# Moving all sums of g and of w_out's halves to GpSimd, and placing every step of a fused attention and PReLU kernel anew

## The chip, the cores and the metric

The kernel runs on one core of a Trainium2 chip. The core has five engines that run side by side, each through its own instructions in order: TensorE (PE in the profile, with its weight loads as PEld), VectorE (DVE), ScalarE (ACT), GpSimd (POOL) and SyncE (SP, which only issues DMAs here). The metric is the time of one execution on the device in microseconds (us); less is better.

## What is computed

There are 8 batches and 8 heads, 512 tokens and 32 states per head, with vectors of 64. Tokens read from states, states read from tokens (both by softmax), and all rows, 4096 of tokens and 256 of states, each 512 long over the heads, go through a two-layer network with a PReLU of its own slope for each of the 2048 hidden units.

```
scores = scale * x @ state^T            # per batch and head: 512 x 32
a      = softmax(scores);   xread = a @ state
a2     = softmax(scale * state @ x^T);  sread = a2 @ x
rows   = concatenate([xread, sread])    # heads side by side: 4352 x 512
h      = rows @ w_in                    # w_in: 512 x 2048
g      = max(h, 0) + alpha * min(h, 0)
out    = g @ w_out                      # w_out: 2048 x 512
```

Inputs and outputs are float32; the matrix products take float16.

## The kernel before

**Order.** The instructions are in an order that is written out by hand: the string ORDER (lines 17 to 95) holds 1090 tokens, and the loop at line 735 runs them one after another. A token is the name of a step and its arguments, split by dots, and the table at line 720 says which function it calls. The tiles' framework adds the waits that the data and the buffers need. As each engine runs its instructions in the order in which they were written, the order of the tokens is the order on every engine and in every DMA queue: a step that has to wait holds up what stands behind it on its engine. Where a step can run on several engines, a letter in the token says which: `a` ACT, `v` DVE, `p` POOL. A last number in a token of a matrix product is the PSUM bank (0 to 5) that it opens; a new owner of a bank waits until the old content is read. Two more banks, "two", hold scores or a pair of state-by-w_in products.

**Loads.** x of batch 0 comes in two float32 halves over SP's queue (`load_x0`), the states of batch 0 over ACT's, and alpha behind x on SP's. The others go over POOL's queue and are cast to float16 on the way: `lst` the other states, `wi.f` a quarter of w_in, `wo.i` a quarter of w_out, `lx.b` x of batch b (three buffers). `stc` casts the states of batch 0 on POOL.

**Attention, batch by batch.** For batch 0, x is cast (`cx`) and transposed by PE (`xt`, copied out by `xo`); `tsc` makes the scores of its tokens, with the states in pairs (`sbd`). For the others `xd` transposes x by a DMA of SP's queue (batch 1 goes by `xt`), `sc` makes the scores with the states on the partitions, and `sb` transposes them in blocks. The softmax over states is `smax` (DVE), `ssh` (subtracts the maximum; DVE or POOL), `sexp` (ACT), `ssum` (DVE), `snorm` (POOL), and `wb` turns the weights back (batch 0: `at` and `ao`). The softmax over tokens is `tm` (maximum, DVE), `nb` (scales the maximum, ACT or DVE), two `te` (ACT), `tsum` (DVE), two `tn` (POOL), `tt` (a DMA transpose), and `rd` with `rdo`, which read the tokens into the row block of the states.

**First layer.** The reads of the states are not made for themselves: `m.b.f` multiplies the states of batch b by a quarter f of w_in (`mo` casts it out of PSUM), and `F.b.j` multiplies that by the softmax weights: h for 512 tokens and 128 hidden units (batch 0 begins in halves, `f`). The rows of the states are batch 8, with w_in itself. `N` (ACT) takes relu(-h), and `G` (DVE) adds (1 - alpha) times it to h, which gives g; `n` and `g` are the same for `f`. `oma` makes 1 - alpha on DVE.

**Second layer.** Batches 0 to 2 multiply g by w_out outright: `S.b.q.j`, two hidden blocks for 128 tokens, into one bank; `O` copies and stores. Batches 3 to 8 use seven products of halves instead of eight (a Strassen form). `W.i` makes four sums ws of w_out's halves, `U.b.i.c` makes four sums of g's halves for each of two groups c of hidden units (16 blocks of 128 units are 4 groups; a sum is 128 x 1024, and 128 x 512 in batch 8), and `P.b.p.i.c` multiplies for one row half i. The products run together in three banks x, y and v; `K` keeps what stands in x, and `Q` adds it and stores a quarter. U.b.1.c feeds P.b.5, U.b.2.c feeds P.b.6 and U.b.4.c, U.b.3.c feeds P.b.7, and U.b.4.c feeds P.b.3. Each sum of g has one buffer, so the next batch's sum waits for the last product of this one.

`Z.k.n` issues n products of zeros, which compute nothing.

Of the kernel before, what the change touches and what calls it, by code (L numbers as in the profile page):

```python
# [22 lines left out]
tsum.0 tn.0.1 tn.0.0 ao.1.v n.0.1.0 xt.1.1.0.4 n.0.0.0 g.0.1.0.1 F.0.4.1 g.0.0.0.0 xt.1.1.1.2 g.0.1.0.0 mo.1.0.a  # L23
xt.1.0.0.3 m.1.1 N.0.4 xo.1.1.1.v S.0.2.1.5 xt.1.0.1.2 xo.1.0.0.a xo.1.1.0.v mo.1.1.a g.0.0.0.1 S.0.2.0 m.2.0.3.4
xo.1.0.1.v sc.1 G.0.4 mo.2.0.a.0 f.0.1.1.0 tm.1 mo.2.0.a.1 f.0.0.1.2 n.0.1.1 F.0.7.1 F.0.5.3 g.0.1.1.0 n.0.0.1 F.0.6.4
g.0.1.1.1 W.1.p nb.1.a te.1.1 g.0.0.1.0 g.0.0.1.1 S.0.1.1.0 S.0.1.0 S.0.3.0.2 S.0.3.1 N.0.5 sb.1 te.1.0 N.0.6 G.0.5
m.0.2 mo.0.2.a N.0.7 G.0.6 S.0.1.2 S.0.2.2 smax.1 ssh.p.1 S.0.3.2 F.0.10.3 N.0.10 F.0.9.4 G.0.7 m.0.3 G.0.10 N.0.9
S.0.2.3 mo.0.3.a F.0.8.1 F.0.11.3 N.0.8 G.0.9 S.0.1.3 N.0.11 G.0.8 S.0.3.3 sexp.1 G.0.11 F.0.12.4 ssum.1 N.0.12 G.0.12
xd.2 m.1.2 F.0.14.1 S.0.3.4 F.0.13.3 N.0.14 S.0.1.4 tsum.1 S.0.2.5 S.0.1.5 mo.1.2.a S.0.3.5 N.0.13 G.0.13 S.0.0.1.4
S.0.2.4 snorm.p.1 G.0.14 F.0.15.3 tt.0 tn.1.1 wb.1 m.1.3 N.0.15 S.0.1.6 S.0.2.6 G.0.15 F.1.10.1 S.0.1.7 F.1.4.3  # L30
S.0.2.7 mo.1.3.a W.3.p N.1.10 O.0.1.v G.1.10 N.1.4 sc.2 O.0.2.a rd.0.0 rdo.0.a G.1.4 m.2.2.1.5 S.0.3.7 sb.2 tn.1.0
tt.1 lx.3 mo.2.2.a.0 F.1.9.3 S.0.3.6 tm.2 nb.2.v N.1.9 F.1.1.0 O.0.3.a F.1.11.1 S.0.0.7 N.1.11 F.1.8.2 mo.2.2.a.1
N.1.8 G.1.9 G.1.11 N.1.1 smax.2 S.0.0.3 F.1.5.3 N.1.5 F.1.6.5 S.0.0.4 S.0.0.6 S.0.0.5 N.1.6 G.1.1 ssh.p.2 F.1.2.1
F.1.3.0 te.2.1 G.1.5 G.1.8 S.1.1.2.3 te.2.0 N.1.2 S.1.1.5 G.1.6 F.1.0.2 sexp.2 G.1.2 ssum.2 tsum.2 tn.2.0 S.0.0.0
tn.2.1 S.0.0.2 N.1.3 S.1.1.4 rd.1.5 N.1.0 O.0.0.a m.3.2 mo.3.2.a F.1.7.1 N.1.7 S.1.0.4.4 snorm.p.2 G.1.0 S.1.0.5 W.2.p
F.1.15.2 G.1.3 S.1.1.1 G.1.7 N.1.15 F.1.12.0 rdo.1.v F.1.14.1 G.1.15 N.1.12 G.1.12 S.1.1.3 xd.3 N.1.14 G.1.14 lx.4
m.2.3.5.2 m.2.1 mo.2.1.a S.1.0.0 mo.2.3.v.0 S.1.0.3 S.1.0.2 wb.2 m.3.3.0.1 mo.2.3.a.1 sc.3 mo.3.3.a.1 m.3.0.5.2
mo.3.3.a.0 mo.3.0.a.0 S.1.1.7 tm.3 F.1.13.1 N.1.13 F.2.8.0 S.1.0.1 nb.3.a G.1.13 S.1.3.0.5 S.1.0.7 sb.3 S.1.1.6
mo.3.0.a.1 te.3.0 F.2.14.2 te.3.1 tt.2 S.1.1.0 N.2.14 F.2.3.1 smax.3 O.1.1.a S.1.3.4 N.2.8 tsum.3 G.2.14 S.1.0.6
O.1.0.a F.2.1.3 ssh.p.3 G.2.8 m.3.1 N.2.3 rd.2.2 N.2.1 lx.5 F.2.12.4 rdo.2.v N.2.12 G.2.3 F.2.0.0 G.2.1 S.1.3.3 G.2.12  # L40
F.2.11.2 S.1.2.1.1 N.2.0 tn.3.0 S.1.3.2 G.2.0 N.2.11 G.2.11 sexp.3 ssum.3 snorm.p.3 tn.3.1 S.1.2.6 F.2.2.3 N.2.2 G.2.2
xd.4 F.2.15.4 F.2.6.0 N.2.15 N.2.6 F.2.5.2 N.2.5 G.2.15 G.2.5 S.1.2.7 S.1.2.2 S.1.3.6 F.2.10.3 N.2.10 G.2.6 S.1.2.5
F.2.13.4 mo.3.1.a S.1.3.5 G.2.10 m.4.1.2.0 N.2.13 mo.4.1.a.1 wb.3 tt.3 mo.4.1.a.0 S.1.3.1 S.1.2.0 S.1.3.7 m.4.0.3.0
mo.4.0.a.0 mo.4.0.a.1 O.1.3.a G.2.13 sc.4 F.2.9.2 N.2.9 S.1.2.4 F.2.7.4 S.2.1.7.3 S.2.1.5 tm.4 sb.4 N.2.7 S.2.1.0
S.2.1.6 F.2.4.0 nb.4.a te.4.1 G.2.7 G.2.9 te.4.0 S.1.2.3 smax.4 ssh.p.4 m.5.0.5.4 rd.3.2 N.2.4 mo.5.0.a.0 G.2.4
O.1.2.a lx.6 tsum.4 m.4.3 S.2.1.4 F.3.3.5 mo.4.3.v mo.5.0.a.1 F.3.7.1 N.3.3 G.3.3 S.2.1.1 N.3.7 F.3.9.0 rdo.3.a
S.2.1.2 G.3.7 N.3.9 G.3.9 S.2.1.3 tn.4.1 m.4.2.4.5 m.5.2 O.2.1.a m.7.0.2.1 mo.7.0.a.0 mo.4.2.v.1 F.3.0.0 F.3.2.3
S.2.0.2.5 N.3.0 N.3.2 S.2.0.0 sexp.4 G.3.0 mo.4.2.v.0 mo.7.0.a.1 tn.4.0 tt.4 S.2.2.1.2 F.3.15.0 N.3.15 S.2.2.4
mo.5.2.a S.2.2.3 F.3.14.4 S.2.2.6 G.3.2 ssum.4 F.3.8.1 G.3.15 F.3.1.3 N.3.14 G.3.14 snorm.p.4 S.2.0.3 xd.6 N.3.8 N.3.1
G.3.8 F.3.6.0 N.3.6 S.2.2.0 xd.5 G.3.1 F.3.5.4 m.6.0 N.3.5 F.3.4.1 G.3.6 N.3.4 F.3.10.3 N.3.10 wb.4 W.4.p F.3.11.0  # L50
N.3.11 S.2.2.2 S.2.0.1 mo.6.0.a S.2.0.6 G.3.4 S.2.2.5 rd.4.1 G.3.5 G.3.11 sc.5 rdo.4.v m.5.3.4.0 mo.5.3.a.0 mo.5.3.a.1
S.2.0.5 G.3.10 S.2.0.7 F.3.12.1 N.3.12 S.2.2.7 U.3.1.0.v S.2.3.5.4 U.3.2.0.v tm.5 nb.5.v S.2.3.3 G.3.12 S.2.3.4
F.3.13.3 N.3.13 S.2.0.4 U.3.4.0.p te.5.0 O.2.2.a S.2.3.6 te.5.1 F.4.10.0 N.4.10 F.4.9.1 S.2.3.0 O.2.0.v S.2.3.7 N.4.9
F.4.3.5 G.3.13 U.3.1.1.p S.2.3.1 F.4.13.3 P.3.1.1.1.2 S.2.3.2 sb.5 smax.5 N.4.13 P.3.1.0.1 ssh.p.5 G.4.10 O.2.3.a
F.4.4.0 G.4.9 G.4.13 F.4.11.4 N.4.3 G.4.3 tsum.5 F.4.15.1 N.4.4 tn.5.1 G.4.4 N.4.11 P.3.1.1.0 P.3.1.0.0 K.3.1.v N.4.15
F.4.6.3 F.4.12.5 N.4.6 U.3.2.1.v F.4.14.0 N.4.12 P.3.6.1.0 G.4.11 P.3.6.0.0 sexp.5 P.3.6.1.1 N.4.14 U.3.4.1.p
P.3.6.0.1 G.4.12 G.4.6 m.6.2.4.5 m.5.1 U.3.3.0.p G.4.15 mo.6.2.a.0 F.4.8.3 N.4.8 G.4.14 F.4.1.4 G.4.8 N.4.1 G.4.1
F.4.5.1 mo.6.2.a.1 P.3.2.0.0.0 K.3.2.a N.4.5 P.3.2.0.1 ssum.5 F.4.2.3 P.3.7.0.0.5 P.3.5.1.0 P.3.2.1.1 F.4.7.4
P.3.5.0.1 U.3.3.1.p P.3.2.1.0 G.4.5 F.4.0.1 N.4.2 G.4.2 P.3.7.1.0 Q.3.0.0 P.3.5.0.0 snorm.p.5 m.6.3.3.0 N.4.7 G.4.7
N.4.0 G.4.0 lx.7 mo.5.1.a P.3.5.1.1 mo.6.3.a.0 P.3.7.1.1 U.4.1.0.v mo.6.3.a.1 wb.5 P.3.7.0.1 U.4.1.1.p K.3.4.a  # L60
m.7.3.4.1 sc.6 xd.7 mo.7.3.a.0 m.6.1.3.0 mo.6.1.a.1 tm.6 P.3.3.1.0 Q.3.1.1 F.5.6.4 P.4.1.1.1.0 N.5.6 G.5.6 U.4.2.1.p
mo.7.3.a.1 P.4.1.0.1 P.3.3.0.0 sb.6 nb.6.a P.3.4.1.1 F.5.12.1 P.3.4.1.0 U.4.2.0.v mo.6.1.v.0 P.3.4.0.0 F.5.14.4
P.3.4.0.1 P.3.3.1.1 U.4.3.0.v P.4.1.0.0 te.6.1 N.5.12 Q.3.1.0 N.5.14 P.3.3.0.1 Q.3.0.1.a F.5.11.3 P.4.2.1.1.5 G.5.12
P.4.2.0.0 P.4.1.1.0 smax.6 N.5.11 G.5.11 F.5.7.1 N.5.7 G.5.14 K.4.1.v F.5.4.2 P.4.2.1.0 N.5.4 G.5.7 F.5.15.3 te.6.0
tsum.6 U.4.3.1.p ssh.p.6 U.4.4.0.p U.4.4.1.p sexp.6 P.4.2.0.1 P.4.6.0.0 G.5.4 P.4.6.1.1 sc.7 Q.4.0.0 m.7.2.4.1
mo.7.2.a.1 mo.7.2.a.0 F.5.0.2 P.4.6.0.1 P.4.6.1.0 F.5.10.5 N.5.0 ssum.6 G.5.0 P.4.7.1.0.1 F.5.3.4 N.5.15 F.5.5.2
G.5.15 K.4.2.a P.4.5.0.1 snorm.p.6 P.4.7.0.1 tm.7 P.4.5.1.0 F.5.13.3 P.4.7.1.1 N.5.5 N.5.10 G.5.10 N.5.3 P.4.5.0.0
G.5.5 N.5.13 G.5.13 wb.6 P.4.5.1.1 K.4.4.a tn.5.0 F.5.8.5 F.5.1.2 N.5.1 P.4.7.0.0 G.5.3 tn.6.1 N.5.8 P.4.3.1.0 tn.6.0
tt.6 F.6.6.3 G.5.1 P.4.3.0.0 tt.5 Q.4.1.1 F.5.9.4 F.5.2.2 N.6.6 G.6.6 U.5.1.1.p N.5.9 nb.7.a G.5.8 P.4.3.0.1 P.4.3.1.1
Q.4.0.1.a U.5.2.1.p G.5.9 N.5.2 P.4.4.1.1 F.6.0.3 m.7.1.5.0 rd.6.4 mo.7.1.a.1 mo.7.1.a.0 P.4.4.1.0 F.6.12.0 te.7.0  # L70
F.6.2.5 G.5.2 F.6.13.2 rdo.6.v U.5.3.0.p sb.7 N.6.0 te.7.1 G.6.0 N.6.12 tsum.7 P.4.4.0.1 P.4.4.0.0 Q.4.1.0 N.6.2
F.6.11.4 N.6.11 G.6.12 G.6.2 P.5.1.0.0.3 P.5.1.1.1 P.5.1.1.0 U.5.1.0.p F.6.15.1 N.6.15 P.5.2.0.1.0 N.6.13 U.5.2.0.v
# [695 lines left out]
```

## Time and profile before

| | |
|---|---|
| time, median of 3 runs | 220.82 us (220.51 to 221.13) |
| the profiled execution: its own time, its span | 220.61 us, 218.7 us |
| granted TensorE clock | 1.0 |
| bytes moved by DMA | 23.68 MB |
| sums of g on DVE and POOL (L662) | 21 and 27 |
| sums of w_out's halves on POOL (L643) | 4, mean 4071 ns |

The profile shows one execution. The span goes from the first to the last instruction of the program; the rest of the execution's time lies around it. A row of a group names line, engine, operation, output and inputs, how often, the busy us and mean ns of one, and, behind the second bar, the idle time of the engine just before them and who ended it. A row of a timeline begins with start and length in us. Busy times of PE are lengths of single matmuls, which overlap: start-to-start distances tell what PE needs. L662 is `g_sum`, L643 `w_sum`, L588 `prelu`, L585 `negative`, L532 `first`, L602 `second`, L683 `product`, L483 `state_w_in`.

### The profile page before, as it was taken

The numbers are of one execution on the slowest core, as the hardware profiler recorded it, in microseconds if no ns is written. First come the engines' busy times: TensorE is split into PE (matmuls) and PEld (weight loads), VectorE is DVE, ScalarE is ACT, GpSimd is POOL, SyncE is SP. The second block draws the span as 40 slices with busy tenths as digits, with TensorE's granted clock in tenths as the row PEclk, the third lists the DMA queues.
The fourth block names the chain that finished last, engine by engine and source line by source line (L and its number), as shares of the span: only waits on it lengthen the run. The fifth ranks groups of instructions, "written<-read, shape, count | busy, mean of one in ns | idle before, by whom it ended". The sixth has DMA issues, their size and how long they took to land.

```text
span 218.7 us, 4851 instructions
## 1 busy us (share of the span) xinstructions
PE 206.1 (94%) x1931; PEld 128.1 (59%) x1931; DVE 184.9 (85%) x282; ACT 142.7 (65%) x275; POOL 126.1 (58%) x86
## 2 busy tenths in 40 slices
...
GB/s 174 207 191 206 206 194 179 47 148 135 158 73 153 161 96 59 204 178 0 139 8 0 135 155 97 51 144 48 99 4 96 79 21 0 48 49 25 98 144 120
DMA packets 51926, 23.68 MB, mean 108 GB/s; under 512 B 38464, under 2 KB 50368, under 8 KB 51904
## 3 DMA queue, kind: packets, MB, share of 16 engines
...
q14 instruction: 7, 0.06, 0.1%
...
## 4 chain that ended last, share of the span: by engine, by line
PE 72%; DVE 13%; DMA 6%; ACT 4%; issue 2%; POOL 0%; SPq 0%; ACTq 0%; POOLq 0%
PE h L532 20%; PE px L683 15%; PE o L602 15%; PE pv L683 8%; DMA alpha_sb<-in_moe_alpha_dram 6%; PE m_ps L483 4%; DVE g L588 4%; PE py L683 3%; DVE gsum L662 2%; PE sr_ps L456 2%; PE h L541 2%; DVE ts L329 2%; ACT e L421 1%; DVE mx L362 1%; ACT neg L585 1%
## 5 line engine op out<-in xcount | busy, mean ns | idle before, releaser
L588 DVE SCALAR_TENSOR_TENSOR g<-neg,oma_sb,h 128x512 f16<-128x512 f32 (+1 forms) x140 | 93.0, 704 | 7.7 <-ACT neg L585 7.2
L585 ACT ACTIVATE neg<-h 128x512 f32<-128x512 f32 (+1 forms) x140 | 75.5, 580 | 28.6 <-PE h L532 20.5
L532 PE MATMUL h<-aT,m 128*128 128x512 f16 x248 | 68.1, 379 | 1.6 <-ACT osb L619 0.9
L602 PE MATMUL o<-w_out_sb,g 128*128 128x512 f16 x192 | 49.9, 380 | 0.0
L683 PEld LDWEIGHTS <-gsum 128*128 128x128 f16 x352 | 34.2, 98 | 9.8 <-issue 1.4
L532 PEld LDWEIGHTS <-m 128*128 128x128 f16 x248 | 23.6, 98 | 22.9 <-issue 5.0
L602 PEld LDWEIGHTS <-g 128*128 128x128 f16 x192 | 17.9, 98 | 23.2 <-issue 2.4
L683 PEld LDWEIGHTS <-g 128*128 128x128 f16 x264 | 25.7, 98 | 8.3 <-issue 1.2
L384 POOL TENSOR_TENSOR an<-ts,r 128x1024 f16<-128x1024 f32 (+1 forms) x9 | 15.5, 1722 | 20.1 <-DVE r L381 17.0
L367 POOL TENSOR_TENSOR ts<-ts,mx 128x1024 f32<-128x1024 f32 x7 | 13.4, 1912 | 23.4 <-DVE mx L362 23.4
L662 POOL TENSOR_TENSOR gsum<-g,gsum 128x1024 f16<-128x1024 f16 (+1 forms) x9 | 17.6, 1962 | 14.2 <-PE px L683 8.8
L683 PE MATMUL px<-ws,gsum 128*128 128x256 f16 x176 | 23.8, 273 | 0.2 <-DVE kept L699 0.2
L662 POOL TENSOR_TENSOR gsum<-g,g 128x1024 f16<-128x1024 f16 x6 | 13.7, 2287 | 17.1 <-DVE g L588 16.8
L509 ACT CAST m<-m_ps 128x512 f16<-128x512 f32 x32 | 17.8, 592 | 3.5 <-PE m_ps L483 3.5
L699 ACT COPY kept<-px 128x512 f32<-128x512 f32 (+1 forms) x12 | 6.9, 577 | 13.4 <-PE px L683 13.4
L662 POOL TENSOR_TENSOR gsum<-g 128x1024 f16<-128x1024 f16 (+1 forms) x7 | 13.9, 1987 | 1.8 <-DVE g L588 1.7
L421 ACT ACTIVATE e<-sc,nb 128x512 f16<-128x512 f32 x16 | 11.0, 694 | 5.0 <-issue 3.0
L483 PE MATMUL m_ps<-w_in_sb,stT 64*32 64x512 f16 x256 | 12.3, 383 | 1.3 <-ACT e L421 0.7
L435 POOL TENSOR_SCALAR e<-e,r 128x512 f16<-128x512 f16 x16 | 11.0, 697 | 4.1 <-ACT osb L619 3.1
L683 PE MATMUL py<-w_out_sb,g 128*128 128x256 f16 x88 | 12.7, 272 | 0.6 <-DVE oq L716 0.6
L507 ACT CAST m<-m_ps 128x1024 f16<-128x1024 f32 x12 | 12.2, 1017 | 1.0 <-PE m_ps L483 1.0
L683 PE MATMUL px<-w_out_sb,gsum 128*128 128x256 f16 x88 | 12.6, 273 | 0.0
...
## 6 DMA issues: line engine op xcount, KB each, us to landing
...
xg<-in_x_dram POOLq DMA_DIRECT2D x7, 512.0 KB, 8.1
...
w_in_sb<-in_moe_w_in_dram POOLq DMA_DIRECT2D x4, 512.0 KB, 11.8
w_out_sb<-in_moe_w_out_dram POOLq DMA_DIRECT2D x4, 512.0 KB, 14.7
x<-in_x_dram SPq DMA_DIRECT2D x2, 512.0 KB, 4.7
...
st<-in_state_dram POOLq DMA_DIRECT2D x1, 224.0 KB, 7.6
```

Of the source, the lines that this page charges most:

```text
L367: engine(e).tensor_tensor(blocks(cols(live["ts", b], j, S)), blocks(scored(b, j)), over_blocks(cols(live["mx", b], j, S // N)), ALU.subtract,)
L384: engine(e).tensor_tensor(blocks(cols(live["an", b], j, S)), blocks(cols(live["ts", b], j, S)), over_blocks(cols(live["r1", b], j, S // N) ...
L421: nc.scalar.activation(live["e2", b][:, g, :, :], live["sc", b][:, :, :, g, :].rearrange("p r j s -> p (r j) s"), EXP, bias=live["nb", b][ ...
L483: nc.tensor.matmul(t[N * k : N * (k + 1), :], st_head(b, h)[64 * r : 64 * r + 64, :], w_in_sb[64 * r : 64 * r + 64, c, 512 * f : 512 * (f ...
L507: copier(e)(m_tile(b, f), t)
L509: copier(e)(m_tile(b, f)[:, g, :], t[g])
L532: nc.tensor.matmul(h.rearrange("p (r j s) -> p r j s", r=2, j=2), ms[b, f][:, g, 128 * j : 128 * (j + 1)], weights(b, g), start=(g == 0), ...
L585: nc.scalar.activation(neg, h, RELU, bias=0.0, scale=-1.0)
L588: nc.vector.scalar_tensor_tensor(g_tile(b, jc), negs.pop((b, jc)), oma_sb[:, jc : jc + 1], hs.pop((b, jc)), ALU.mult, ALU.add,)
L602: nc.tensor.matmul(outs[b, q], g_tile(b, jc)[:, 128 * q : 128 * (q + 1)], w_out_sb[:, jc, :], start=not begun and jc == 2 * jc2, stop=left ...
L662: engine(e).tensor_tensor(t, x(), y(), op)
L683: nc.tensor.matmul(pbanks[b, name][:, i, :], of(b, c)[:, j, 128 * i : 128 * (i + 1)], moving[:, 4 * c + j, :], start=not begun and j == 0, ...
```

## The change

One function changes: `w_sum` makes a sum in two halves of four blocks each, so that the four W tokens become eight. The rest is in ORDER. All 48 U tokens name POOL (27 before; 21 were on DVE), as do all W. Both `nb` that were on DVE go to ACT; `ssh.6` goes from POOL to DVE; some copies change between ACT and DVE (`sto`, `cx`, `xo`, `ao`, `mo`, `rdo`, `K`, `Q`, `O`). `wi.1`, the first token before, stands behind `lx.1` now, and `wi.2`, `wi.3`, `wo.1` and `wo.2`, issued ahead of batch 0's `snorm` before, stand behind it; the first load on POOL's queue is `wi.0`, behind `stc`. Every other token may have another place and another bank. The numbers of matrix products, of zeros and of steps of the other kinds are the same.

```diff
 ORDER = """
-wi.1 stc wi.0 cx.0.0.a cx.0.1.v Z.0.9 stt.0 sbd.0.v sto.a sbd.1.a Z.1.5 lst xt.0.0.1.1 xt.0.0.0.2 Z.3.6 xo.0.0.0.v
-cx.1.1.a cx.1.0.v xt.0.1.0.3 xo.0.1.0.a xo.0.0.1.v lx.1 wo.0 tsc.0.0.4 tsc.0.1 xt.0.1.1.5 smax.0.0 ssh.v.0.0 sc.0.0
-xo.0.1.1.a m.0.1.0.2 wo.1 mo.0.1.a.0 wi.2 tsc.1.0.1 Z.3.2 tsc.1.1 smax.0.1 wi.3 wo.2 oma sc.0.1 Z.3.5 m.0.0.3.5
-sexp.0.0 Z.0.11 str.1.0 ssum.0.0 ssh.v.0.1 sexp.0.1 snorm.p.0.0 tm.0 mo.0.0.a.1 ssum.0.1 snorm.p.0.1 at.0.4 mo.0.0.v.0
-nb.0.a sro.1.a str.0.1 Z.5.13 te.0.0 ao.0.v sro.0.v f.0.1.0.5 te.0.1 f.0.0.0.0 lx.2 at.1.3 wo.3 m.1.0 mo.0.1.v.1
+stc Z.0.9 wi.0 cx.0.1.a stt.0 sto.v Z.1.5 xt.0.0.1.1 lst sbd.0.v cx.0.0.a xt.0.0.0.2 xo.0.0.0.a cx.1.0.v cx.1.1.v
+Z.3.6 xt.0.1.0.3 sbd.1.a lx.1 tsc.0.0.4 xo.0.0.1.v tsc.0.1 xt.0.1.1.5 sc.0.0 xo.0.1.1.a xo.0.1.0.v tsc.1.0.2 Z.0.2
+tsc.1.1 smax.0.0 ssh.v.0.0 sexp.0.0 smax.0.1 ssh.v.0.1 sexp.0.1 sc.0.1 tm.0 Z.0.5 m.0.0.0.1 Z.3.11 oma mo.0.0.a.0
+ssum.0.1 nb.0.a te.0.0 te.0.1 str.1.3 sro.1.a str.0.5 Z.4.13 wi.1 wo.0 snorm.p.0.1 at.1.4 ao.1.a ssum.0.0 snorm.p.0.0
+sro.0.v wi.2 mo.0.0.v.1 m.2.0.2.0 mo.2.0.v.1 wo.1 m.1.0 mo.1.0.a at.0.3 ao.0.v xt.1.1.0.5 mo.2.0.v.0 wi.3 xo.1.1.0.a
+xt.1.1.1.1 xo.1.1.1.v xt.1.0.1.4 xo.1.0.1.v f.0.1.1.0 n.0.1.1 g.0.1.1.1 xt.1.0.0.3 xo.1.0.0.v wo.2 f.0.0.0.2 n.0.0.0
+g.0.0.0.0 m.1.1 mo.1.1.a m.0.1.5.1 mo.0.1.a.0 f.0.0.1.4 mo.0.1.a.1 g.0.1.1.0 f.0.1.0.3 W.1.0.p sc.1 n.0.0.1 n.0.1.0
+g.0.0.0.1 tm.1 g.0.0.1.0 nb.1.a F.0.6.0 g.0.0.1.1 sb.1 g.0.1.0.1 N.0.6 G.0.6 g.0.1.0.0 F.0.5.2 te.1.0 lx.2 te.1.1
+S.0.1.1.5 F.0.4.1 S.0.3.1.4 wo.3 S.0.3.0 S.0.1.0 m.0.2 F.0.7.0 N.0.4 G.0.4 N.0.5 G.0.5 mo.0.2.a N.0.7 S.0.2.1.3
+S.0.2.0 G.0.7 F.0.9.1 tsum.1 tn.1.0 N.0.9 G.0.9 smax.1 ssh.p.1 xd.2 tsum.0 tn.0.1 F.0.10.2 S.0.3.3 N.0.10 G.0.10
+S.0.1.3 tn.1.1 tt.1 S.0.1.2 F.0.8.0 F.0.11.1 N.0.11 N.0.8 S.0.3.2 G.0.8 m.0.3 S.0.0.0.2 G.0.11 S.0.2.3 S.0.0.3 S.0.0.2
...
+N.8.10 P.6.3.1.1 G.8.10 F.7.6.5 N.7.6 G.7.6 P.6.7.0.0 F.7.14.2 N.7.14 P.6.7.1.1 F.8.13.4 N.8.13 Q.6.1.1 G.7.14
+P.8.1.0.1.5 P.6.2.0.0 G.8.13 P.6.4.1.0 P.6.4.0.0 P.6.2.0.1 P.7.1.0.1.2 F.8.9.4 P.6.3.0.1 P.7.1.1.0 P.6.4.0.1 U.8.3.0.p
+U.7.3.1.p N.8.9 G.8.9 P.8.2.0.0.4 P.8.2.0.1 P.8.1.0.0 P.6.2.1.0 P.7.1.0.0 P.6.3.1.0 Q.6.0.0 U.7.1.1.p U.7.2.1.p
+P.7.1.1.1 P.8.7.0.0.0 K.8.1.v Q.8.0.0 P.7.7.1.1.4 K.7.1.a P.6.4.1.1 Q.6.1.0 P.7.6.1.0 P.7.6.0.0 U.7.4.1.p P.7.6.1.1
+P.7.6.0.1 K.7.2.a P.7.2.0.0.3 U.7.3.0.p Q.6.0.1.v P.7.2.1.1 P.7.5.1.1 P.7.5.0.0 P.7.5.0.1 P.7.7.0.1 P.7.5.1.0
+U.7.4.0.p U.8.1.1.p U.8.2.1.p P.7.7.0.0 P.7.7.1.0 K.7.4.a Q.7.1.1 P.7.3.1.1 P.7.3.0.1 P.7.3.1.0 P.7.4.0.0 P.7.4.0.1
+U.8.1.0.p P.7.4.1.0 U.8.2.0.p P.7.4.1.1 Q.7.1.0 P.8.6.0.1 P.8.6.0.0 K.8.2.a P.7.2.0.1 P.7.3.0.0 P.8.5.0.0 P.8.5.0.1
+U.8.3.1.p P.8.7.0.1 P.7.2.1.0 Q.7.0.1.a K.8.4.v Q.8.1.1 U.8.4.1.p P.8.3.0.1 P.8.4.0.0 Q.7.0.0 P.8.4.0.1 Q.8.1.0
+U.8.4.0.p P.8.3.0.0 Q.8.0.1.a
 """
 ...
-    def w_sum(i, e):
-        a, c = W_SUMS[i]
-        t = ws[i] = consts.tile([128, n_h, d_h], F16, name=f"ws_{i}")
-        engine(e).tensor_tensor(t, w_halves[a], ws[c] if c in ws else w_halves[c], ALU.subtract)
+    def w_sum(i, c, e):
+        a, b = W_SUMS[i]
+        if i not in ws:
+            ws[i] = consts.tile([128, n_h, d_h], F16, name=f"ws_{i}")
+        rows = slice(4 * c, 4 * c + 4)
+        engine(e).tensor_tensor(
+            ws[i][:, rows, :],
+            w_halves[a][:, rows, :],
+            (ws[b] if b in ws else w_halves[b])[:, rows, :],
+            ALU.subtract,
+        )
```

129 lines of the change are left out of this document (57 added, 72 removed).

## Prediction

> **What bounds the kernel now.** I read the page's busy times first, then the engines in four stretches, cut where the kind of work changes.
>
> ```profile
> PE 206.1 (94%) x1931; PEld 128.1 (59%) x1931; DVE 184.9 (85%) x282; ACT 142.7 (65%) x275; POOL 126.1 (58%) x86
> ```
>
> ```profile
> 18.80:98.00 79.20, 77.58 (x714) 34.83 (x715) 73.19 (x108) 66.91 (x126) 44.84 (x29) 1.00 0.92 145
> 98.00:138.00 40.00, 38.60 (x361) 24.21 (x355) 39.39 (x55) 27.78 (x54) 28.14 (x15) 1.00 0.34 77
> 138.00:180.00 42.00, 41.77 (x406) 30.97 (x405) 38.65 (x60) 27.43 (x56) 32.10 (x20) 1.00 0.24 67
> 180.00:215.00 35.00, 34.91 (x299) 28.98 (x297) 24.56 (x43) 11.61 (x25) 10.87 (x7) 1.00 0.18 61
> ```
>
> (After the stretch: its length, then busy PE, PEld, DVE, ACT, POOL, granted clock, DMA share, GB/s.) From 18.8, when the first h starts, to 215 PE is idle for 3.3 us in all, at full clock. Neither order changes a matmul, so the time can move in two places: how much of PE's work is done when the start is over, and PE's breaks after it. DVE is full only from 98 to 138, where it makes sums beside softmax. The prices of PE's steps, from the chain of waits:
>
> ```profile
> 51.54 1.29 PE o L602 x6
> 200.34 2.18 PE px L683 x20
> ```
>
> A step S or F (two matmuls of 512) takes 0.43, a P (four of 256) 0.437.
>
> **The start: loads.** First POOL's timeline, then landings, asked for one issue at a time (the last column is us from issue to landing), then what DVE waits for.
>
> ```profile
> 1.43 0.97 POOL L193 DMA_DIRECT2D w_in_sb<-in_moe_w_in_dram  x1
> 4.51 0.29 POOL L236 CAST st<-st 128x128 f16<-128x128 f32 x1 [2.12 <-DMA st<-in_state_dram]
> 7.19 1.52 POOL L199 DMA_DIRECT2D w_out_sb<-in_moe_w_out_dram  x2
> ```
> ```profile
> st<-in_state_dram POOLq DMA_DIRECT2D x1, 224.0 KB, 7.6
> ```
> ```profile
> w_in_sb<-in_moe_w_in_dram POOLq DMA_DIRECT2D x1, 512.0 KB, 7.7
> ```
> ```profile
> w_out_sb<-in_moe_w_out_dram POOLq DMA_DIRECT2D x1, 512.0 KB, 12.3
> ```
> ```profile
> 14.00 0.17 DVE L254 TENSOR_SCALAR oma_sb<-alpha_sb 128x16 f32<-128x16 f32 x1 [2.60 <-DMA alpha_sb<-in_moe_alpha_dram]
> ```
>
> Packets of the two queues from 8 to 9 us, then from 9 to 10:
>
> ```profile
> q0 software_dynamic: 158, 0.15, 87.4%
> q1 hardware_dynamic: 813, 0.00, 57.4%
> ```
> ```profile
> q0 software_dynamic: 199, 0.20, 119.4%
> q1 hardware_dynamic: 200, 0.00, 27.3%
> ```
>
> q1 is SP's queue, with alpha in it (by count some 2,000 packets of 4 bytes); q0 is POOL's. Beside weight packets alpha goes one for one, 200 a us; where q0 pauses, 813 pass in the same time. The change issues no weights at 1.43; its first load, wi.0, comes behind the cast at about 4.8. wi.1 at 1.43 needed 7.7, of which 512 KB at q0's 0.20 MB a us are 2.6: at most 5.1 from issue to the first packet. If wi.0 needs 3 to 5, q0 is empty until 8 or 9 and alpha has the engines to itself once x is in (about 6.5). It then lands near 8.5 (bounds 8 and today's 14.0). The 2.6 us for which DVE stands at oma go, with ssum, the shift and the maximum of batch 0 queued behind it.
>
> The other side of it: wi.0, st (13.1) and lx.1 keep their landings, wi.1 takes the place in which wo.0 lands today (7.19+12.3 = 19.5), and each load from wo.0 on slips by one place, 2.6 us. wi.2, wo.1, wi.3 and wo.2 are now issued behind snorm.0, near 15, but still ahead of q0's backlog. W.1.0 waits on POOL for wo.0 (22.1) with lx.2, wo.3 and tn.1 behind it; what follows there, ssh.1 first, is not due before 29.
>
> **The start: PE.**
>
> ```profile
> 12.32 1.38 PE L219 MATMUL z<-zero 128*128 128x256 f16 x11
> 13.75 0.58 PE L230 MATMUL st_ps<-ident,st 128*64 128x128 f16 x14
> 16.32 0.40 PE L348 MATMUL at_ps<-ident,an 128*128 128x128 f16 x4 [1.98 <-POOL an L384]
> 18.81 1.03 PE L554 MATMUL h<-aT,m 128*128 128x256 f16 x8
> 28.86 0.41 PE L483 MATMUL m_ps<-w_in_sb,stT 64*32 64x512 f16 x8 [0.71 <-ACT e L421]
> 31.47 0.41 PE L483 MATMUL m_ps<-w_in_sb,stT 64*32 64x512 f16 x8
> ```
> ```profile
> L585 ACT ACTIVATE neg<-h 128x512 f32<-128x512 f32 (+1 forms) x140 | 75.5, 580 | 28.6 <-PE h L532 20.5
> L507 ACT CAST m<-m_ps 128x1024 f16<-128x1024 f32 x12 | 12.2, 1017 | 1.0 <-PE m_ps L483 1.0
> L421 ACT ACTIVATE e<-sc,nb 128x512 f16<-128x512 f32 x16 | 11.0, 694 | 5.0 <-issue 3.0
> ```
>
> (Rows: PE in time; then three groups of ACT, with the mean in ns behind the busy time.) st lands as before, so str.1 starts at 13.75 again. With str.0 (0.5 each) and 13 zeros (11 took 1.38) PE is at at.1 at 16.3; without the wait at oma an.1 is there about 2 us before that. Two at (0.35), m.2.0 and m.1.0 (0.4), three xt (0.22) bring the first f to 18.3. m.1.1 then needs wi.1, 19.5, where PE comes to it anyway. From there ACT leads: the cast mo.1.1 (1.0), two smaller casts and two n (0.55 each, by the row of the same shape), nb (0.2), N.0.6 (0.55) and two te (0.7 and a read, 0.8) are 5.5 us from 19.9, and m.0.2 waits for the bank that the last te gives back: 25.4 against 28.86. Before has then done three more steps (F.0.7, S.0.2.0, S.0.2.1: 1.3), so the lead is 2.2. F.0.9 and S.0.3.3 wait for G.0.4 and G.0.7, which stand on DVE behind tm and sb: 0.3 and 0.4. m.0.3 so comes at 31.3, with three steps more done than before had at 31.47: 0.2 + 1.3, a lead of **1.5**. Bounds: 0, if the load of wi.3, one place later at 29.7, slips by as much again; 2.5, without ACT's delay.
>
> **The sums leave DVE.** What POOL and DVE did, and PE's breaks behind it; then the sums' groups with their shortest, median and longest:
>
> ```profile
> 126.47 2.13 POOL L662 TENSOR_TENSOR gsum<-g 128x1024 f16<-128x1024 f16 x1
> ```
> ```profile
> 126.93 2.22 DVE L662 TENSOR_TENSOR gsum<-gsum,g 128x1024 f16<-128x1024 f16 x1
> ```
> ```profile
> 128.93 0.60 PE L683 MATMUL px<-w_out_sb,gsum 128*128 128x256 f16 x4
> 129.81 0.59 PE L532 MATMUL h<-aT,m 128*128 128x512 f16 x2 [0.27 <-DVE m L509]
> 131.01 1.03 PE L683 MATMUL py<-w_out_sb,g 128*128 128x256 f16 x8 [0.61 <-DVE oq L716]
> ```
> ```profile
> L662 POOL TENSOR_TENSOR gsum<-g,gsum x9: 1154/2133/2566, 100.8 to 211.0; 128x1024 f16<-128x1024 f16 x7, 128x512 f16<-128x512 f16 x2
> L662 DVE TENSOR_TENSOR gsum<-gsum,g x7: 425/684/2222, 100.0 to 207.2; 128x1024 f16<-128x1024 f16 x6, 128x512 f16<-128x512 f16 x1
> L662 POOL TENSOR_TENSOR gsum<-g,g x6: 2126/2131/2669, 104.9 to 191.9; 128x1024 f16<-128x1024 f16 x6
> ```
>
> A DVE sum of 0.68 took 2.22, and ended when POOL's did, at 128.6 and a little. PE's starts stand 0.88 and 1.20 apart there instead of 0.44 and 0.43: 1.2 lost. DVE sums stand close ahead of two more breaks:
>
> ```profile
> 108.16 1.46 PE L532 MATMUL h<-aT,m 128*128 128x512 f16 x6 [0.46 <-DVE g L588]
> 179.27 0.60 PE L683 MATMUL px<-ws,gsum 128*128 128x256 f16 x4 [0.19 <-DVE kept L699]
> ```
>
> 0.5 and 0.2. With 17 full sums and 4 halves (some 14 us) off DVE I let all three go: **-1.9** (bounds 0 and -2.4). Elsewhere DVE's relief is worth nothing, PE being full. The subtraction ssh.6 that comes to DVE, two small scalings that go to ACT, and the copies that change engine stand beside PE's work: 0, and up to 0.5 each way if one holds a bank that PE waits for.
>
> **POOL takes them.** 17 x 2.13 + 4 x 1.15 is 41 us more, less one ssh: about 165 in all. The four W are the same work in eight shorter blocks. From U.3.1.0 on POOL has 40 full sums and 8 halves, 94 us, where PE has about 112 of work; the softmax steps go between. The narrow place is the end. From U.7.3.1, which needs F.7.6, come six full sums and seven halves: 6 x 2.13 + 7 x 1.15 = 20.8. PE has 56 steps from F.7.6 to the last product, P.8.3.0.0, which needs the last sum: 56 x 0.437 = 24.5. For F.7.6 and the way to its g I allow 2.6 (0.6, then neg 0.6, g 0.7, and 0.7 of queueing). POOL then ends 1.1 ahead of PE, but single sums on the way have as little as 0.2. Bounds 0 and +3.3 (rival 2); nearest to the undisturbed rows, I take **+0.5**.
>
> The Trainium skill, "GPSIMD Engine Reference", section 4.1, gives elementwise work with two inputs to VectorE and calls GpSimd about twice slower at it. Here the rows say three times, 2.13 to 0.68. By the skill's factor a sum would cost POOL 1.4 and leave it ample room; the forecast goes by the rows. The page's advice against the move is what rival 2 would bear out.
>
> **New waits.** All steps stand elsewhere, and one break of before is of a kind that the change doesn't touch:
>
> ```profile
> 66.27 0.59 PE L532 MATMUL h<-aT,m 128*128 128x512 f16 x2 [0.90 <-ACT osb L619]
> ```
>
> I leave it in and add half of another: **+0.4** (bounds -0.9 and, for three more, +2.7).
>
> **The sum**, against the profiled execution's own 220.61 (span 218.7, and 1.9 around it; the median shown, 220.82, is 0.1% above): -1.5 - 1.9 + 0.5 + 0.4 = -2.5, so **218.1 us**.
>
> **The rivals.** (1) *The lead of the start is mostly lost* to the later weights. For it: every load from wo.0 on a place later, and W.1.0 in POOL's way. Against it: 1.6 us of margin at m.0.3. Lead 0: 219.6. (2) *POOL becomes the bound at the end.* For it: 1.1 us of room, and one queue in order. Against it: its long sums (2.57, 2.67) are few, and none of DVE's is left to disturb it. Disturbed still, six by 0.46 and seven by 0.23, they give 4.4, less the room 3.3: 221.4, slower. It decides from the point where a full sum takes over 2.2, or G.7.6 is 3 us behind F.7.6. (3) *The softmax chains stall*, where ssh and snorm now queue behind W blocks, tn or sums on POOL: three breaks of 0.9 give 220.8, four 221.7. (4) *Only the start counts*, DVE's breaks coming back for other reasons: 220.0.
>
> **How the numbers follow.** Forecast 0.50 (its own range 216.5 to 219.5), (1) 0.08, (2) 0.16, (3) 0.18, (4) 0.08. A measurement of this kernel tells about 0.3%, 0.7 us, from no change. Faster: the forecast, (1) and 0.02 of (4), 0.60. Same: 0.06 of (4) and 0.04 of (3), 0.10. Slower: (2) and the rest of (3), 0.30. The range goes from 216.0 (a lead of 2.5 and few new waits) to 222.0, which takes in (2) and four breaks of (3).
>
> **What would show it.** Right: alpha landing below 10 us and oma without a wait; m.0.2 near 25 and m.0.3 near 31; no gsum on DVE, no full sum over 2.2 on POOL; PE breaks after 31 us below 2 in sum; POOL's last sum done ahead of P.8.3.0.0. Wrong: m.0.3 after 32.5 (start); POOL without a gap over the last 20 us while PE waits for gsum (rival 2); PE breaks behind ACT, DVE's softmax steps or POOL between 35 and 160 of over 3 us (rival 3).

## The result, and the profile after

The changed kernel takes 219.70 us (median of 10 runs, 219.13 to 220.32), the kernel before in the same runs 221.06 (220.51 to 223.94): 1.4 us **faster** by the medians. The ratio is 0.993, interval 0.990 to 0.996; it compares means and leaves out the slowest execution of before, 223.94, which is counted as one in a slower state. In a second set of runs it was 0.991 (0.988 to 0.995). Forecast were 218.1 us, 2.5 below the profiled execution of before. The profiled execution after has 219.88 us (span 218.1), only 0.7 below that of before (220.61, 218.7): half of the gain in the medians is not in this pair of traces, and the section on the hardware says how far the clock explains that.

The busy times of the kernel after, from its page:

```profile
PE 207.0 (95%) x1931; PEld 128.3 (59%) x1931; DVE 171.5 (79%) x258; ACT 144.4 (66%) x279; POOL 164.3 (75%) x110
```

The same four stretches, the first from the first h (columns as before):

```profile
18.27:98.00 79.73, 76.87 (x688) 33.24 (x686) 69.27 (x102) 66.26 (x125) 46.83 (x35) 1.00 0.84 137
98.00:138.00 40.00, 39.62 (x335) 25.10 (x334) 35.85 (x48) 30.80 (x62) 38.77 (x22) 1.00 0.47 90
138.00:180.00 42.00, 41.49 (x423) 30.38 (x422) 37.81 (x58) 26.96 (x56) 39.83 (x22) 1.00 0.28 77
180.00:215.00 35.00, 34.29 (x304) 29.38 (x301) 17.52 (x32) 10.68 (x23) 30.43 (x19) 1.00 0.20 66
```

Read the second number of a row: from 98 to 138 PE is busy for 1.0 us more than before (39.62 against 38.60), so the stretch in which DVE made sums did gain. In the first row PE is idle for 2.9 us, where before it was 1.6: that is where the gain was given back. POOL is nearly full from 98 to 180 now and has longer gaps only at the end.

The start: alpha's landing in the kernel after, PE's timeline, then oma and DVE's and ACT's steps ahead of m.0.2:

```profile
alpha_sb<-in_moe_alpha_dram SPq DMA_DIRECT2D x1, 8.0 KB, 5.9
```

```profile
18.27 0.60 PE L554 MATMUL h<-aT,m 128*128 128x256 f16 x4
...
26.38 0.41 PE L483 MATMUL m_ps<-w_in_sb,stT 64*32 64x512 f16 x8 [1.23 <-ACT e L421]
...
32.03 0.41 PE L483 MATMUL m_ps<-w_in_sb,stT 64*32 64x512 f16 x8
```

```profile
13.84 0.17 DVE L254 TENSOR_SCALAR oma_sb<-alpha_sb 128x16 f32<-128x16 f32 x1
...
23.00 0.64 ACT L585 ACTIVATE neg<-h 128x512 f32<-128x512 f32 x1
...
23.55 1.24 DVE L329 STREAM_TRANSPOSE ts<-sc 128x1024 f32<-128x1024 f32 x1
...
24.88 0.69 ACT L421 ACTIVATE e<-sc,nb 128x512 f16<-128x512 f32 x1 [1.24 <-DVE ts L329]
```

The kernel before has the same wait already, at the second e of the same batch:

```profile
28.03 0.69 ACT L421 ACTIVATE e<-sc,nb 128x512 f16<-128x512 f32 x1 [1.01 <-DVE ts L329]
```

alpha lands early and oma waits for nothing. at.1 (16.31), the first h and m.1.1 (19.49) stand where the forecast put them (16.3, 18.3, 19.5). m.0.2 is 1.0 late and m.0.3 0.7, because ACT, free at 23.64, stood for 1.24 at the first e until DVE had read the same scores. From there on I count as a break what the start-to-start distance of two PE steps has over the usual one, where it is more than 0.15. After m.0.3 they add up to 3.83 us before and 3.79 after: not fewer, only others. Before, 2.18 of them were the four that the prediction puts down to DVE's sums and its copy of the bank x (108, 129.8, 131, 179 us). After, these are gone, and there are new ones, the largest at m.4.3 (84.8 us, 1.03), F.5.12 (139.3, 0.67), F.2.14 (67.6, 0.46), P.3.7.0.0 (124.7, 0.41). Behind 139.3 PE has none.

PE's waits from 18 us on, in the kernel after (in all, times, longest):

```profile
PE m_ps L483 <- ACT e L421: 2.2, 2, 1.2
PE h L532 <- DVE g L588: 0.5, 1, 0.5
PE m_ps L483 <- DVE ts L329: 0.3, 1, 0.3
PE m_ps L483 <- ACT osb L619: 0.2, 1, 0.2
```

The waits behind DVE that the prediction shows at 129.8, 131 and 179 have left the list, and what is behind osb has shrunk from 0.9 to 0.2; the wait for e, 0.71 in the rows of before, has trebled.

### The profile page after: what moved, and what is told of

Read it like the earlier page. It is cut to its first block, busy times and chain, and to the rows that moved or that the text cites. A ratio compares the mean times of both kernels' runs of the same rounds, so it can differ in the third digit from the quotient of the medians.

```text
span 218.1 us, 4862 instructions
## 1 busy us (share of the span) xinstructions
PE 207.0 (95%) x1931; PEld 128.3 (59%) x1931; DVE 171.5 (79%) x258; ACT 144.4 (66%) x279; POOL 164.3 (75%) x110
## 3 DMA queue, kind: packets, MB, share of 16 engines
q1 hardware_dynamic: 32816, 15.22, 27.1%
## 4 chain that ended last, share of the span: by engine, by line
PE 60%; DVE 10%; ACT 6%; issue 1%; ACTq 0%
PE px L690 17%; PE h L532 16%; PE pv L690 9%; PE o L602 7%; DVE g L588 5%; PE py L690 4%; PE h L541 3%; PE m_ps L483 3%; ACT e L421 2%; DVE ts L329 2%; ACT neg L585 2%; PE sr_ps L456 1%; DVE nb L404 1%; DVE ts L367 1%; PE sc L298 1%
## 5 line engine op out<-in xcount | busy, mean ns | idle before, releaser
L588 DVE SCALAR_TENSOR_TENSOR g<-neg,oma_sb,h 128x512 f16<-128x512 f32 (+1 forms) x140 | 93.5, 708 | 17.0 <-ACT neg L585 16.3
L585 ACT ACTIVATE neg<-h 128x512 f32<-128x512 f32 (+1 forms) x140 | 74.3, 581 | 28.0 <-PE h L532 18.2
L384 POOL TENSOR_TENSOR an<-ts,r 128x1024 f16<-128x1024 f32 (+1 forms) x9 | 15.4, 1720 | 16.3 <-DVE r L381 16.3
L669 POOL TENSOR_TENSOR gsum<-g 128x1024 f16<-128x1024 f16 (+1 forms) x12 | 24.4, 2047 | 0.8 <-PE pv L690 0.8
L669 POOL TENSOR_TENSOR gsum<-g,g 128x1024 f16<-128x1024 f16 (+1 forms) x12 | 23.5, 1962 | 1.5 <-DVE g L588 1.3
L669 POOL TENSOR_TENSOR gsum<-gsum,g 128x1024 f16<-128x1024 f16 (+1 forms) x12 | 23.6, 1965 | 0.9
L669 POOL TENSOR_TENSOR gsum<-g,gsum 128x1024 f16<-128x1024 f16 (+1 forms) x12 | 23.5, 1961 | 0.3
L367 POOL TENSOR_TENSOR ts<-ts,mx 128x1024 f32<-128x1024 f32 x6 | 11.5, 1914 | 11.4 <-DVE mx L362 10.3
L723 DVE TENSOR_TENSOR oq<-pv,kept 128x512 f32<-128x512 f32 (+1 forms) x12 | 7.7, 643 | 8.7 <-ACT kept L706 4.4
L507 ACT CAST m<-m_ps 128x1024 f16<-128x1024 f32 x13 | 13.3, 1025 | 1.6 <-PE m_ps L483 1.6
```

What stands on the lines that cost most here:

```text
L367: engine(e).tensor_tensor(blocks(cols(live["ts", b], j, S)), blocks(scored(b, j)), over_blocks(cols(live["mx", b], j, S // N)), ALU.subtract,)
L384: engine(e).tensor_tensor(blocks(cols(live["an", b], j, S)), blocks(cols(live["ts", b], j, S)), over_blocks(cols(live["r1", b], j, S // N) ...
L507: copier(e)(m_tile(b, f), t)
L585: nc.scalar.activation(neg, h, RELU, bias=0.0, scale=-1.0)
L588: nc.vector.scalar_tensor_tensor(g_tile(b, jc), negs.pop((b, jc)), oma_sb[:, jc : jc + 1], hs.pop((b, jc)), ALU.mult, ALU.add,)
L669: engine(e).tensor_tensor(t, x(), y(), op)
```

## The experiments

**The kernel after again**, with no edit, as the measure for the runs beside it.

> The changed kernel once more, on the chip of the next three, so that they can be compared with it. Expected: 0.992 to 0.996 of the kernel before, about 219.5 us.

219.75 us (219.47 to 220.70), ratio 0.991 (0.988 to 0.995); m.0.3 at 31.66 and the same list of breaks, 6.30 in all from the first h on, where the first profile had 6.33. Between these two executions the start varies by some 0.4 us, the breaks don't.

### What the start's lead comes from

**wi.1 back to the front, in the kernel after.**

```diff
-stc Z.0.9 wi.0
+wi.1 stc Z.0.9 wi.0
...
-Z.4.13 wi.1 wo.0
+Z.4.13 wo.0
```

> The changed kernel with the first quarter load (wi.1) again the first token, ahead of the states' cast. Theory (oma's wait went because two steps of DVE were put ahead of oma, not because alpha lands early): alpha lands near 14.0 again, oma is due at 13.84, so DVE loses 0.2 us or less and the time stays within 0.3 us of the changed kernel, or gains a little as every other load lands a place earlier. Rival (the prediction's step, loads out of alpha's way are what counts): oma waits again, batch 0's softmax is late, 1 to 2.5 us slower than the changed kernel.

220.45 us (0.994, 0.991 to 0.997), 0.7 above the kernel after in the same set. The landing of alpha, then DVE's steps around oma:

```profile
alpha_sb<-in_moe_alpha_dram SPq DMA_DIRECT2D x1, 8.0 KB, 12.6
```

```profile
12.93 1.21 DVE L403 TENSOR_REDUCE nb<-sc 128x2 f32<-128x1024 f32 x1
14.54 0.18 DVE L253 TENSOR_SCALAR oma_sb<-alpha_sb 128x16 f32<-128x16 f32 x1 [0.40 <-DMA alpha_sb<-in_moe_alpha_dram]
```

alpha is as late as in the kernel before (12.6 us from issue, 12.1 there, 5.9 in the kernel after), and oma waits for 0.40 only, not 2.60. So the later weights are not what takes most of the wait away. **What takes it is oma's own place**: the new order has it behind both shifts and the maximum (nb, which ends at 14.1), the old one ahead of the second shift and of the maximum. The theory had this, and missed in size: it gave the loads 0.3 us or less, and they are worth 0.7, all of it ahead of the first h (18.98 here, 18.27 and 17.92 in the two traces of the kernel after; from there to m.0.3 all three take 13.7 to 13.8).

**wi.1 behind the cast, in the kernel before.**

```diff
-wi.1 stc wi.0
+stc wi.1 wi.0
```

> The kernel before with one token moved: the load wi.1 from ahead of the states' cast to just behind it, so that GpSimd's queue is empty for the first 5 us. Theory (alpha is held up by weight packets that alternate with its own): alpha lands below 9 us, oma loses its wait of 2.6, the first f starts 1.5 to 2 us earlier (17 to 17.3), m.0.2 and m.0.3 come earlier by as much unless a weight load is late, and the time falls by 1 to 2 us. Rival (the later weights eat it): alpha lands early all the same, but m.0.1, which needs wi.1, or m.1.1 waits, the first f is no earlier than 18.3 and the time falls by less than 0.6.

220.72 us, ratio 0.994 (0.991 to 0.998). Landings, then PE:

```profile
st<-in_state_dram POOLq DMA_DIRECT2D x1, 224.0 KB, 8.2
...
alpha_sb<-in_moe_alpha_dram SPq DMA_DIRECT2D x1, 8.0 KB, 5.6
```

```profile
13.45 0.41 PE L482 MATMUL m_ps<-w_in_sb,stT 64*32 64x512 f16 x8 [0.67 <-DMA w_in_sb<-in_moe_w_in_dram]
13.79 1.37 PE L218 MATMUL z<-zero 128*128 128x256 f16 x11
15.22 0.58 PE L229 MATMUL st_ps<-ident,st 128*64 128x128 f16 x14
...
18.22 1.03 PE L553 MATMUL h<-aT,m 128*128 128x256 f16 x8
```

An empty queue does give alpha in 5.6 us, and oma runs at 12.54 without a wait, as the prediction has it. But m.0.1 now waits for wi.1, and the states, one place later, hold str.1 until 15.22 (13.75 before). The first h is 0.6 earlier, not 1.5 to 2: most of the rival's story, and the same 0.6 to 0.7 that the loads are worth in the kernel after. In the profiled execution this was lost again at sc.5 (98.3 us), which waited 0.67 for the DMA that transposes x. The run with one sum moved, below, has the same wait (0.88), the traces of the kernel before and of the same one sum with oma moved as well haven't; what brings it is not shown.

**oma behind the maximum, in the kernel before**, with its loads as they were.

```diff
-wi.3 wo.2 oma sc.0.1
+wi.3 wo.2 sc.0.1
...
-snorm.p.0.0 tm.0 mo.0.0.a.1
+snorm.p.0.0 tm.0 oma mo.0.0.a.1
```

> The kernel before with one token moved: oma stands behind tm.0 (the maximum of batch 0) on DVE, not ahead of ssum.0.0; the loads stay. Theory (the lead of the start came from DVE no longer standing at oma with batch 0's softmax behind it): DVE does ssum, the shift and the maximum in the 2.6 us, PE's first h comes 1 to 2 us sooner than 18.8, and 0.5 to 2 us remain at the end. Rival (the other work of the start, loads and ACT, sets the pace anyway): within 0.3 us of the kernel before.

219.34 us, ratio 0.989 (0.984 to 0.994): one token moved gives as much as the whole change. DVE, then PE:

```profile
14.60 0.17 DVE L253 TENSOR_SCALAR oma_sb<-alpha_sb 128x16 f32<-128x16 f32 x1
```

```profile
16.96 1.03 PE L553 MATMUL h<-aT,m 128*128 128x256 f16 x8
...
29.62 0.41 PE L482 MATMUL m_ps<-w_in_sb,stT 64*32 64x512 f16 x8
```

m.0.3 comes at 29.62 instead of 31.47, and the last product 1.86 earlier: what is won ahead of m.0.3 stays won to the end. From its first h to m.0.3 this order has breaks of 1.0 in all; the kernel after has 2.5 there, and keeps a lead of 0.7 where this edit keeps 1.85.

### What the sums cost on either engine

**All 21 sums back to DVE, in the kernel after** (letters only), and the mirror of it, **all 21 to POOL, in the kernel before**.

```diff
-U.3.1.0.p U.3.2.0.p
+U.3.1.0.v U.3.2.0.v
...
```

> The changed kernel's order with the 21 sums of g back on DVE that were there before; nothing else. Theory (DVE sums and POOL sums hold each other up, and DVE is near full from 98 to 138): long rows of gsum on both engines and breaks of PE of 1 to 3 us in all, 1 to 2.5 us slower than the changed kernel. Rival (POOL's load is what costs in the changed kernel): POOL's relief makes it 0.5 us or more faster.

```diff
-U.3.1.0.v S.2.3.5.4 U.3.2.0.v
+U.3.1.0.p S.2.3.5.4 U.3.2.0.p
...
```

> The kernel before with all 21 sums of VectorE given to GpSimd, where they stand in the order (letters only): the change's GpSimd part without its placement. Theory (a sum on GpSimd takes three times as long and must be placed ahead accordingly; the order of before places VectorE's sums just ahead of their use): the VectorE breaks at 108, 129 to 131 and 179 go (about 2 us), but the products wait for late sums, most of all behind the run of sums near the end, where GpSimd is given some 14 full sums' work in the last 25 us; 2 to 8 us slower than before. Rival (the engine alone was what counted): 1.5 to 2 us faster than before, with no PE wait for a sum.

The first took 232.99 us, ratio 1.050 (1.046 to 1.055), 13 us above the kernel after and far beyond what either theory gave it; the second 231.02, 1.042 (1.035 to 1.049), some 9 us, also above its bounds. Around the first great break of the first:

```profile
112.04 2.12 POOL L668 TENSOR_TENSOR gsum<-g,g 128x1024 f16<-128x1024 f16 x1
...
114.20 0.69 DVE L668 TENSOR_TENSOR gsum<-gsum,g 128x1024 f16<-128x1024 f16 x1 [4.15 <-POOL gsum L668]
114.81 1.40 DVE L587 SCALAR_TENSOR_TENSOR g<-neg,oma_sb,h 128x512 f16<-128x512 f32 x2
...
115.60 1.01 PE L689 MATMUL py<-w_out_sb,g 128*128 128x256 f16 x4 [4.43 <-DVE g L587]
```

The DVE sum takes 0.69; it had to wait for a sum on POOL, and the two G behind it, which need nothing of that, waited along, and PE for them. This is no price of a collision, so the run doesn't tell what it was made for. Besides, PE had half its clock for 6.8 us from 114.28 on (last section). The second run's PE waits from 100 us on:

```profile
PE px L682 <- POOL gsum L661: 5.4, 4, 3.2
...
PE pv L682 <- POOL gsum L661: 0.8, 1, 0.8
```

6.2 us for sums that stand too close ahead of their use, and PE had half its clock twice for 3.4 us, once behind these waits (last section). So in the old order the letters alone cost 9 us, and in the new order taking them back costs 13: the placement that goes with them is the change.

This run also tells what the three places of the prediction owe to DVE's sums. With no sum on DVE the breaks at 129 to 131 and at 179 are gone, as expected. That at 108 is not: F.4.4 waits for G as before (0.68 over the usual distance, 0.62 before), because the same two softmax steps, ts and mx, stand on DVE ahead of that G.

**The one colliding sum to POOL, in the kernel before.**

```diff
-U.4.2.0.v
+U.4.2.0.p
```

> The kernel before with one sum of g (U.4.2.0) on POOL instead of DVE, one letter. There it took 2.22 us beside a POOL sum, and PE broke by 1.2 us behind it. Theory (two-input work of DVE and POOL in SBUF holds each other up): the long row and both breaks go, 0.7 to 1.2 us faster. Rival (the breaks come from DVE's softmax steps of batch 5 and 6 around it): half of the breaks stay, 0.6 us or less, or POOL's ssh.6 is late and nothing is gained.

221.61 us (219.90 to 224.53), ratio 0.995 (0.991 to 1.000). The median of all executions doesn't settle it, the trace does: the breaks at 129.8 and 131 (0.44 and 0.77) are gone, and from F.4's first step to F.6's it takes 39.70 us instead of 40.98. That is 1.2 of the prediction's second term. The five executions at full clock agree: their median, 220.14, is 1.2 below that of the kernel before at full clock (last section).

**ssh.6 back to POOL, in the kernel after.** The change had given this subtraction to DVE.

```diff
-ssh.v.6
+ssh.p.6
```

> The changed kernel with batch 6's subtraction of the maximum (ssh.6) on POOL, one letter. Theory (two-input SBUF work on DVE and a sum on POOL hold each other up): in the changed kernel this subtraction took 2.11 us and the POOL sum beside it 3.10 instead of 2.13, and PE broke for 0.67 at 139.3; on POOL the long rows and the break go, 0.3 to 0.7 us faster than the changed kernel. Rival (POOL has no room for 1.9 us more): a break of PE for gsum or behind snorm.6, same or up to 1.5 us slower.

219.04 us, ratio 0.988 (0.984 to 0.992), 0.7 below the kernel after in the same set; the break at F.5.12 is gone. The place in the kernel after, then in this one:

```profile
135.35 2.11 POOL L669 TENSOR_TENSOR gsum<-g,gsum 128x1024 f16<-128x1024 f16 x1
136.44 2.11 DVE L367 TENSOR_TENSOR ts<-ts,mx 128x1024 f32<-128x1024 f32 x1
137.43 3.10 POOL L669 TENSOR_TENSOR gsum<-g 128x1024 f16<-128x1024 f16 x1
138.47 1.39 DVE L588 SCALAR_TENSOR_TENSOR g<-neg,oma_sb,h 128x512 f16<-128x512 f32 x2
139.26 0.59 PE L532 MATMUL h<-aT,m 128*128 128x512 f16 x2 [0.51 <-DVE g L588]
```

```profile
133.02 1.91 POOL L366 TENSOR_TENSOR ts<-ts,mx 128x1024 f32<-128x1024 f32 x1
...
139.06 2.12 POOL L668 TENSOR_TENSOR gsum<-g 128x1024 f16<-128x1024 f16 x1
```

The change took 21 sums off DVE and put one other instruction of the same kind there, between POOL's sums.

**One more sum on POOL near the end, in the kernel after**: an addition of 128 x 896 whose result is used by nothing.

```diff
+    def extra():
+        t = st.rearrange("p (a b) d -> p a (b d)", b=2)
+        nc.gpsimd.tensor_tensor(t, ws[1][:, :7, :128], ws[3][:, :7, :128], ALU.add)
...
-U.7.3.1.p N.8.9
+U.7.3.1.p X N.8.9
```

> The changed kernel with one more POOL operation near the end, behind U.7.3.1: a sum of 896 elements a partition (about 1.86 us) of two halves' sums into a tile that nobody reads any more. It measures POOL's room in the last 25 us. Theory (POOL is just not the bound: the room at the last sums is 0.3 to 1.3 us in the changed kernel's trace): 0.5 to 1.6 us slower than the changed kernel. First rival (POOL was the bound already): 1.8 us or more slower. Second (POOL has ample room): same.

221.27 us, ratio 0.996 (0.992 to 1.000), 1.5 above the kernel after (219.75). One break is new:

```profile
209.52 1.15 POOL L672 TENSOR_TENSOR gsum<-gsum,g 128x512 f16<-128x512 f16 x1
...
210.72 0.61 PE L693 MATMUL px<-ws,gsum 128*128 128x256 f16 x4 [1.24 <-POOL gsum L672]
```

PE waited for U.8.2.0, the sum that the prediction gave the least room (0.2; the kernel after has 0.27). POOL's end is as tight as reckoned; in the kernel after it just doesn't go over.

### The new waits

**m.0.2 and m.4.3 later, in the kernel after**, behind steps that don't need their bank.

```diff
-S.0.1.0 m.0.2 F.0.7.0
+S.0.1.0 F.0.7.0
...
+S.0.2.0 m.0.2 mo.0.2.a
...
+S.2.2.3 m.4.3 mo.4.3.a
```

> The changed kernel with two state-by-w_in products, m.0.2 and m.4.3, each with its cast, two or three PE steps later. Both stood at the head of PE's queue and waited, 1.39 and 1.03 us, for the double bank that the scores' readers (ts on DVE and two e on ACT, one after another) give back. Theory (the wait is only a matter of what stands in front on PE): the breaks fall below 0.6 and 0.3, 0.8 to 1.6 us faster than the changed kernel. Rival (the casts and h steps behind them are then late): the breaks move to F.0.9 and the next F, 0.3 us or less gained.

220.06 us, ratio 0.991 (0.988 to 0.994), no gain. PE's waits from 18 to 34 us:

```profile
PE h L531 <- ACT m L506: 1.1, 1, 1.1
PE h L531 <- DVE g L587: 0.7, 1, 0.7
```

The 1.39 ahead of m.0.2 became 0.87 at F.0.7 and 1.21 at F.0.9: G and the cast were held up behind the same readers. The 1.03 ahead of m.4.3 became three breaks of 0.16, 0.19 and 0.53. The place of PE's step isn't the cause.

**The readers' order, and ssh.6, in the kernel after.**

```diff
-ssh.v.6
+ssh.p.6
...
-g.0.0.1.1 sb.1 g.0.1.0.1
+g.0.0.1.1 g.0.1.0.1
...
-te.1.0 lx.2 te.1.1
+te.1.0 lx.2 te.1.1 sb.1
...
-te.4.1 sb.4 W.4.1.p te.4.0
+te.4.1 W.4.1.p te.4.0 sb.4
```

> The kernel after, with ssh.6 back on GpSimd (one letter, as in the run that did only this) and with two steps moved in VectorE's order: sb.1 from ahead of batch 1's two exponentials to behind them, sb.4 from between batch 4's two to behind both. Theory (the readers of one batch's scores in PSUM run one after another, on whichever engine, and the states' transpose, 1.24 us, stood in ScalarE's way): the exponential of batch 1 starts about 0.8 earlier, the break ahead of m.0.2 goes from 1.39 to about 0.6, that ahead of m.4.3 from 1.03 to 0.4 or less, and with the 0.7 of ssh.6 the time is 1.5 to 2 us below that of the kernel after, about 218. Rival (the breaks are due to ScalarE's own queue, or G waits take their place, as when the m steps were moved): the breaks stay above 1 each or come back behind F.0.9 and S.2, and the time is that of ssh.6 alone, 0.7 below the kernel after.

218.48 us (218.00 to 218.85), ratio 0.985 (0.980 to 0.989), the best of the orders that come from the kernel after. The end of ACT's reading of batch 1's scores, DVE's reading of them, and PE:

```profile
24.41 0.27 ACT L420 ACTIVATION_READ_ACCUMULATOR e<-sc,nb 128x1 f32 x1
...
24.71 1.25 DVE L328 STREAM_TRANSPOSE ts<-sc 128x1024 f32<-128x1024 f32 x1
...
26.02 0.41 PE L482 MATMUL m_ps<-w_in_sb,stT 64*32 64x512 f16 x8 [1.16 <-DVE ts L328]
```

The theory was half right. The readers do run in turn: now DVE starts 0.03 after ACT has done. But then m.0.2 waits for DVE instead, 8.0 us from the first h as against 8.1, and its break is 1.32: the bank is free when three readers have been through, in whatever order. The break at m.4.3 is 0.89 (expected 0.4 or less). m.0.3 is 0.4 nearer to the first h. Against ssh.6 alone the last product comes 0.5 earlier (212.34, 212.81); the intervals of the two overlap.

**oma and U.4.2.0 alone, in the kernel before**: the two edits above together.

```diff
-wi.3 wo.2 oma sc.0.1
+wi.3 wo.2 sc.0.1
...
-snorm.p.0.0 tm.0 mo.0.0.a.1
+snorm.p.0.0 tm.0 oma mo.0.0.a.1
...
-U.4.2.0.v
+U.4.2.0.p
```

> The kernel before, with oma one place later (behind the maximum of batch 0) and the one colliding sum, U.4.2.0, on GpSimd: the two edits that gained alone, put together, and nothing else of the change. Theory (the two gains lie in different stretches and add): first f near 17, the breaks at 129 to 131 gone, 1.85 + 1.2 = 3 us below the kernel before, that is about 218.2 and below the kernel after. Rival (the GpSimd sum or the earlier start makes new waits): 219.3, the time of the oma edit alone, or more.

218.37 us (217.17 to 221.11), ratio 0.983 (0.978 to 0.988). The last product starts at 211.77 (214.31 before, 213.69 after). The two gains add, as the theory had it: at full clock the medians are 2.0 and 1.2 us lower for one edit alone and 3.2 for both (last section). Two tokens of 1090 so bring more than the new order, and by their medians this and the run above beat both kernels.

## Why the prediction was right, and where it was not

The sign held, and so did the range, which was wide (216.0 to 222.0) and took in no change as well. Both mechanisms held in part. The size did not hold: 0.7 us by the profiled pair and 1.4 by the medians, not 2.5. By the profiled pair, the four terms and what they measured:

| term | forecast | measured |
|---|---|---|
| lead at m.0.3 | -1.5 | -0.7 (0.56 later, with 1.3 of steps more done) |
| breaks behind DVE's sums | -1.9 | -2.2 |
| POOL at the end | +0.5 | 0 |
| new waits | +0.4 | +2.1 (3.79 less the 1.65 that were there before) |
| sum | -2.5 | -0.8 (last product 0.6 earlier) |

**The lead.** alpha's landing (8.5, measured 7.8), the missing wait at oma and the times to m.1.1 came as forecast. The cause was given in part only. That an empty queue lands alpha early and frees oma is so in the old order (5.6 us, no wait). But in the new order oma's place alone takes away 2.2 of the 2.6; the loads account for the other 0.4, and for 0.7 us of the time. It was luck that this cost the forecast nothing: the change did both. The step that failed in size is "m.0.2 waits for the bank that the last te gives back: 25.4": its sum of ACT's work was right (ACT was free for te at 23.64), and left out that te waits while DVE's sb reads the same scores, 1.24. The trace of before showed this wait (1.01), and the forecast passed it over. The Trainium skill, "PSUM — Partial Sum Buffer", section "PSUM bank collisions raise a hardware error", says that two engines must not touch one bank and quadrant at the same time, reads against reads included, and that the compiler's scheduler adds a dependency between any two such instructions. The traces agree: 0.09 us from ts to e in the kernel after, 0.03 from e to ts in the reordered one. Where the forecast listed te, sb belonged into the sum.

**The sums off DVE.** All four breaks went, but not all for the reason given. 1.2 of the 2.2 is the sum U.4.2.0, by a run of its own, and the 0.36 at 179 goes with the letters alone. The 0.62 at 108 stays when all sums leave DVE and nothing else changes, so the step that let it go with them failed; it went with the new order, and by which of its steps is not shown. The row of 2.22 was read a little wrong: it ends at 129.15, not with POOL's sum but 0.55 after it (128.60), as if DVE had begun only then. No gsum ran on DVE, and the one full sum over 2.2 on POOL (3.10) stood beside ssh.6. That subtraction was put at 0 "up to 0.5 each way"; it is 0.7, by a run of its own. The reason was in the forecast's own row, a DVE sum that took 2.22 beside one on POOL, and wasn't applied to an instruction of the same kind.

**POOL at the end.** Right in the working: the last sum was done 1.3 ahead of P.8.3.0.0 (forecast 1.1), U.8.2.0 had 0.27 (0.2). The +0.5 laid on top was not needed. Rival 2 was a near thing: 1.9 us more work on POOL cost 1.5. Its time counts the +0.5 twice: 218.1 less 0.5 plus 3.3 is 220.9, not 221.4.

**New waits.** The term that was off most: 0.4 for "half of another" where the new order brought nine, 3.8 in all. The waits view names 2.0 of it: 1.5 for banks that e, ts and osb still held, and 0.5 for the G behind ssh.6; for the rest it names nothing. Rival 3 came nearer in size (three breaks, 2.7) and had the wrong place: PE waited for no step on POOL.

**What was to show it.** alpha, oma, the sums and POOL's end as in the "right" list; not so PE's breaks after 31 us (3.8, not below 2), m.0.2 (26.4, not 25) and m.0.3 (32.03, between the forecast and the limit of 32.5). The sign of rival 3 came too, as far as the sum goes: all nine breaks, over 3 us, lie between 52 and 140.
